# RWKV-6 attention and a SiLU block on one core: the fourth unit takes its near-diagonal scores as matmul levels, not elementwise

## The chip, the cores and the metric

The kernel runs on one core of one Trainium2 chip. The metric is the device time in microseconds (us) of the whole program, a median of several runs. The core has five engines that work side by side, each through its own instructions in order: TensorE (matmuls; PE in the profile, its weight loads PEld), VectorE (DVE), ScalarE (ACT), GpSimd (POOL) and SyncE (SP, which issues the transfers here).

## The reference

Two blocks follow each other. The first is a linear attention with a state that decays by a factor for each channel and token:

```python
for t in range(S):                       # B, H, S, D = 4, 8, 768, 48
    cur = np.einsum('bhd,bhe->bhde', u[None] * kt, vt)
    y[:, :, t] = np.einsum('bhd,bhde->bhe', rt, state + cur)
    state = wt[:, :, :, None] * state + np.einsum('bhd,bhe->bhde', kt, vt)
```

Its output, as a matrix x of 3072 tokens by 384 channels, goes through `h = x @ w_in` (384 by 2048), `g = h / (1 + exp(-h))` (SiLU) and `g @ w_out` (2048 by 384). All is in float32.

## The kernel before

**Units.** A unit is a stretch of 128 tokens of two of the four batch rows; there are 12 (`units`, line 66), numbered 0 to 11. For each unit the attention is computed in chunk form: a 128 by 128 matrix of scores for each head, applied to the values, plus the contribution of the state; then the state is brought forward. The result goes to `xt`, and the SiLU block follows: eight `up` steps (line 920, 12 matmul records each, with one ScalarE activation) and seven `quarter` steps (line 977, 16 records each). The quarters are the second product by a scheme with seven half-size products in place of eight; the scheme needs sums of the activations (`sums`, line 967) and of the weights (`weight_sums`, line 963), and every quarter ends in one or two additions on VectorE at line 1000. Quarter results alternate between two PSUM buffers (`p_o`), so quarter x waits for the addition of quarter x-2.

**Scores by levels.** Token t reads token s before it with the product of all decays between them. The 128 tokens are split by halves: at level l (block size 2 to the l) the second half of each pair of blocks reads the first half. A level takes 16 matmul records (`score_products`, line 661), and a masked copy on VectorE for each of two head groups (`keep_masked`, line 676). Before each level, queries and keys are multiplied by the decay products that take them to their block's edge: `grow_queries` (VectorE), `grow_keys` and `start_keys` (GpSimd), with a ScalarE copy, `odd_keys` or `odd_ones`. `product` (line 405) makes the decay products of the levels on GpSimd. From unit 2 on, two levels run as one burst (`burst`, line 743): `prepare` writes the queries of the second level into another buffer, so that 32 records can run together; `keep_level` then does the masked writes and `go_on` grows keys and queries for what follows. `go_on` and `prepare` need the burst's keys, and their GpSimd work is in order behind whatever else GpSimd was given.

**The diagonal.** The scores nearest the diagonal come in one of two ways, chosen by `NPAIR = 3` (line 69):

- Units 0 to 2: only the pair of tokens (2i, 2i+1) is made elementwise. `bonus` (line 420) is three products on GpSimd, `bonus_sum` (line 434) sums them on VectorE and sends them by four small transfers, `bonus_spread` (ScalarE) and `bonus_write` (VectorE) put them into `score`. The levels 1 to 6 are matmuls.
- Units 3 to 11: whole blocks of 8 tokens are made elementwise, so that only levels 3 to 6 are matmuls. `block_bonus` (line 485) has eight steps of products on GpSimd (all recorded as line 487), `block_sum` (line 519) five of sums on VectorE (line 521); `block_move` sends the sums through DRAM, `block_spread` and `block_write` put them into `score`. Keys and queries are grown in place over levels 0 and 1 by `grow_own` (line 629). These units need their tokens' r, k and w in another layout, which `load_rk` (line 131) brings; `ruk` has one buffer, and the products write over the loaded tokens. `load_u` and `make_block_mask` are done once before the first such unit.

**The order of the work.** It is written out by hand. Units 0 to 2 are lists near the end of the function. From unit 3 on, `mix(i)` (line 867) gives 13 groups, and the loop at line 1093 emits a group, then so many steps of the SiLU block as the table `ROOM` says: the seven quarters of unit i-2 first, then the eight up steps of unit i-1. In `mix`, the first elementwise unit (`first`, i = 3) has its own turns and products within itself, and its elementwise products lie between its levels; it makes steps 0 to 3 of unit 4 (`early`) in its last group, and unit 4 (`second`) has sums 0 and 1 and steps 4 and 5 in its own third group. All later units find steps 0 to 3 made before their turns (group 10 of the unit before), and sums 0 and 1 and steps 4 and 5 in the last group of the unit before. `turns` are the transposes of w, k and r on VectorE (line 360); `turn_k` (line 773) turns the keys back on TensorE.

The loads of the unit after next are dealt out over the groups from 10 on in unit 3, and from 3 on in the later ones. All transfers are issued by SyncE, in the order of emission.

Of the kernel before, what the change touches and what calls it, by code (L numbers as in the profile page):

```python
# [38 lines left out]
def kernel(  # L39
# [16 lines left out]
    NL = 7  # L56
    NB = 2
# [8 lines left out]
    units = [(n, b0) for n in range(S // L) for b0 in range(0, B, NB)]  # L66
    NSLOT = 2
    NTOK = 2
    NPAIR = 3
    FIRST = 3  # L70
    BLK = 1 << FIRST

# [58 lines left out]
    def load_rk(i):  # L131

        if i < NPAIR:
            for x, src in enumerate((r, k)):
# [10 lines left out]
    second = []  # L145
# [131 lines left out]
    room = pt.tile([128, 4, DM // 2], F32, name="partial", bufs=1).rearrange("p x d -> p (x d)")  # L277
# [45 lines left out]
    first = {}  # L323
# [127 lines left out]
    at = 768  # L451
# [409 lines left out]
    def both(fn, i, *args):  # L861
        return [(fn, i, b, *args) for b in range(NB)]

    def block_loads(i):
        return [(load_blocks, i, name, g) for name in "wkr" for g in range(4)]

    def mix(i):

        first, second, later = i == NPAIR, i == NPAIR + 1, i > NPAIR
        ahead = i + 1 < len(units)  # L870

        def at(now, *steps):
            return steps if now else ()

        def bonus_steps(j, *steps):
            return [(block_bonus, j, x) for x in steps]

        def sum_steps(j, *steps):
            return [(block_sum, j, x) for x in steps]

        def turns(j):
            return [*both(turn, j, "w"), (product, j, 0), *both(turn, j, "k"), *both(turn, j, "r"), (grow_own, j, 0)]

        def start(j):
            return [*[(product, j, l) for l in range(1, NL)], (grow_own, j, 1)]

        early = bonus_steps(i + 1, 0, 1, 2, 3)
        middle = [*sum_steps(i + 1, 0, 1), *bonus_steps(i + 1, 4, 5)]
        move = [*sum_steps(i, 3, 4), (block_move, i), *at(ahead, (load_rk, i + 1))]
        groups = [[*at(first, *both(turn, i, "w"), (product, i, 0))],  # L890
                  [*at(first, *both(turn, i, "k"), *both(turn, i, "r"), (grow_own, i, 0))],
                  [*at(first, *start(i)), *at(second, *sum_steps(i, 0, 1), *bonus_steps(i, 4, 5))],
                  [(odd_keys, i, 2), (grow_keys, i, 2, False), (grow_queries, i, 2), *at(later, *sum_steps(i, 2))],
                  [(prepare, i, 3), *at(first, *bonus_steps(i, 0, 1, 2, 3)), *at(later, *bonus_steps(i, 6, 7))],
                  [(burst, i, 3), (keep_level, i, 3), *at(first, *sum_steps(i, 0, 1), *bonus_steps(i, 4, 5)), *at(later, *move)],
                  [(keep_level, i, 4), (go_on, i, 4), *at(first, (make_block_mask,), *sum_steps(i, 2), *bonus_steps(i, 6))],
                  [(prepare, i, 5), (reverse_v, i), *at(first, *bonus_steps(i, 7))],
                  [*at(first, *move), *at(later, (block_spread, i), (block_write, i))],
                  [(burst, i, 5), (keep_level, i, 5), *at(first, (block_spread, i)), (keep_level, i, 6), (go_on, i, 6),
                   *at(first, (block_write, i))],  # L900
                  [*at(later and ahead, *early)],
                  [*at(i < len(units) - NB, *both(turn_k, i)), *at(ahead, *turns(i + 1))],
                  [*both(y_state, i), *both(y, i), *both(update, i), *at(ahead, *start(i + 1)), *at(first, *early),
                   *at(later and ahead, *middle), (move_x, i)]]

        loads = block_loads(i + NSLOT) if i + NSLOT < len(units) else []
        if i + 1 < len(units):
            loads.insert(len(loads) // 2, (load_values, i + 1))

        behind = groups[3 if i > NTOK + 1 else 10:]  # L910
        for at, group in enumerate(behind):
            group += loads[at * len(loads) // len(behind):(at + 1) * len(loads) // len(behind)]
        return groups
# [92 lines left out]
    def ups(i):  # L1006

        steps = [[(up, i, m)] for m in range(FC // 2)]
        for m in range(FH // 2 - 1):

            steps[FH // 2 + 1 + m].append((sums, i, m))
        steps[-1].append((sums, i, FH // 2 - 1))
        return steps

    def downs(i):
        return [[(quarter, i, x)] for x in range(7)]

    def do(*steps):
        for fn, *args in steps:
            fn(*args)  # L1020
# [16 lines left out]
    blocks = block_loads(2)  # L1037
# [30 lines left out]
    blocks = block_loads(3)  # L1068
# [6 lines left out]
    for m in range(6):  # L1075
# [4 lines left out]
    blocks = block_loads(4)  # L1080
    do(*blocks[0:2], (level, 2, 2), (prepare, 2, 3), (weight_sums, 1), (down, 0, 1, 0), (down, 0, 0, 3), (down, 0, 1, 1),
       (sums, 1, 0), (bonus, 2, 0), (bonus_sum, 2, 0))
    do(blocks[2], (burst, 2, 3), (keep_level, 2, 3), (keep_level, 2, 4), (go_on, 2, 4), (prepare, 2, 5), (bonus, 2, 1),
       (bonus, 2, 2), (down, 0, 1, 2), (bonus_sum, 2, 1), (load_rk, 3), (load_u,), (sums, 1, 1), *blocks[3:7], (down, 0, 1, 3))
    do((burst, 2, 5), (keep_level, 2, 5), (keep_level, 2, 6), (go_on, 2, 6), (up, 1, 6), (bonus_spread, 2), (bonus_write, 2),
       (load_values, 3), *both(turn_k, 2), (weight_sums, 2), (up, 1, 7), (sums, 1, 2))
    do((sums, 1, 3), *both(y_state, 2), *both(y, 2), *both(update, 2),
       (move_x, 2),
       *blocks[7:])

    ROOM = 1, 1, 1, 2, 2, 1, 1, 1, 2, 1, 1, 1, 0
    assert sum(ROOM[:5]) >= 7
    for i in range(3, len(units)):
        steps = downs(i - 2) + ups(i - 1)
        groups = mix(i)
        if i == NTOK + 1:

            groups[3].insert(0, (weight_sums, 3))
        for group, room in zip(groups, ROOM):
            do(*group)  # L1100
            for step in steps[:room]:
                do(*step)
            steps = steps[room:]
    for step in downs(len(units) - 2) + ups(len(units) - 1) + downs(len(units) - 1):
        do(*step)

# [29 lines left out]
```

## Time and profile before

| | |
|---|---|
| Time, median of 3 runs | 636.34 us (636.14 to 637.03) |
| Span in the profile | 634.8 us, mean granted TensorE clock 0.997 |
| TensorE busy, matmul / weight load | 620.5 us / 561.6 us |
| VectorE, GpSimd, ScalarE busy | 434.4 us, 373.7 us, 185.8 us |
| Chain that ended last | TensorE 80%, GpSimd 9%, transfers 4%, VectorE 3% |
| Up steps (line 925) | 1152 records, 258.1 us |
| Quarters (line 991) | 528 + 508 + 176 records in the three largest groups, 208.3 us |
| Level matmuls with p_sc (line 669) | 496 records, 36.5 us |
| Block products with ruk from tokens (line 487) | 36 records, 56.3 us |

A line of the page's groups has: source line, engine, operation, output and inputs, shape, count; then the busy time in all, the mean of one in ns, and the engine's idle time just before them with what ended it. A timeline line has: start and length in us, engine, line, operation, count, and in brackets the idle time before with its releaser. One row of the slices has 40 equal slices of the span, each digit the busy share in tenths.

### The profile page before, as it was taken

To read this page: it belongs to the slowest core of one execution; us is meant where nothing else is said; L and a number is where in the kernel's file an instruction comes from. 1 tells how busy PE (TensorE), PEld (TensorE's weight loads), DVE (VectorE), ACT (ScalarE), POOL (GpSimd) and SP (SyncE) were. 2 spreads that over 40 slices of the span, in tenths; PEclk is the share of its full clock that TensorE was granted. 3 is DMA by queue.
4 is the path that set the end of the run, shared out by engine and by line. 5 is a ranking of instruction groups with operands and counts; after the bars stand their busy time and mean duration, and the time that the engine had idled before them with its cause. 6 is when DMAs were issued, how large, how long until landed. Compare 5 with 4: busy or idle time off the path is not lost.

```text
span 634.8 us, 12253 instructions
## 1 busy us (share of the span) xinstructions
PE 620.5 (98%) x4574; PEld 561.6 (88%) x4574; DVE 434.4 (68%) x750; ACT 185.8 (29%) x377; POOL 373.7 (59%) x421
## 2 busy tenths in 40 slices
PE   8999999999888999999999999999999999999997
PEld 7888876889788899899889889989989989989997
DVE  7879779885593696696587596497597587561031
ACT  5798881202310321221221221221131122120120
POOL 6998298569469278478278378468458558500000
PEclk9999999999998999999999999999999999999999
DMA  9966864533353643543443442453353222100000
GB/s 216 290 152 167 190 176 50 112 73 65 81 71 55 128 65 52 126 64 51 111 67 52 110 72 49 96 87 51 79 102 53 47 62 52 34 0 26 26 1 25
DMA packets 203292, 53.75 MB, mean 85 GB/s; under 512 B 186465, under 2 KB 194657, under 8 KB 203233
## 3 DMA queue, kind: packets, MB, share of 16 engines
q1 hardware_dynamic: 201648, 52.39, 40.7%
q10 hardware_dynamic: 1584, 0.59, 0.5%
q8 instruction: 36, 0.59, 0.4%
q14 instruction: 24, 0.19, 0.1%
HBM read 43.67 MB, written 5.31 MB: 77 GB/s over the span
## 4 chain that ended last, share of the span: by engine, by line
PE 80%; POOL 9%; DMA 4%; DVE 3%; SPq 2%; issue 1%; ACT 1%; POOLq 0%; DVEq 0%; ACTq 0%
PE p_h L925 36%; PE p_o L991 27%; PE p_sc L669 4%; PE p_m L807 3%; PE p_m L947 2%; PE p_m L669 2%; PE p_m L794 2%; DMA tokens_w<-in_w_dram 2%; POOL ruk L487 2%; POOL tk L625 2%; POOL tw L408 2%; DMA u_bc<-in_u_dram 1%; POOL tk L634 1%; PE p_m L781 1%; PE p_sc L821 1%
## 5 line engine op out<-in xcount | busy, mean ns | idle before, releaser
L925 PE MATMUL p_h<-xt,w_in_sb 128*128 128x256 f32 x1152 | 258.1, 382 | 0.7 <-POOL tk L649 0.7
L925 PEld LDWEIGHTS p_h<-xt,w_in_sb 128*128 128x128 f32 x1152 | 215.9, 190 | 32.6 <-POOL tk L649 0.9
L934 ACT ACTIVATE gt<-p_h 128x512 f32<-128x512 f32 x90 | 53.6, 596 | 248.2 <-PE p_h L925 248.1
L625 POOL TENSOR_TENSOR tk<-tk,tw 128x256 f32<-128x256 f32 x126 | 86.9, 711 | 60.1 <-ACT tk L595 31.3
L991 PE MATMUL p_o<-own,temps 128*128 128x192 f32 x528 | 90.5, 331 | 5.8 <-DVE temps L1000 3.7
L991 PEld LDWEIGHTS p_o<-own,temps 128*128 128x128 f32 x528 | 87.6, 193 | 7.2 <-DVE temps L1000 4.6
L991 PE MATMUL p_o<-w_out_sb,gt 128*128 128x192 f32 x508 | 87.4, 328 | 0.0
L991 PEld LDWEIGHTS p_o<-w_out_sb,gt 128*128 128x128 f32 x508 | 82.7, 190 | 0.9 <-issue 0.4
L487 POOL TENSOR_TENSOR ruk<-tokens_rk 128x768 f32<-128x768 f32 (+1 forms) x36 | 56.3, 1574 | 39.4 <-DMA tokens_rk<-in_k_dram 28.2
L408 POOL TENSOR_TENSOR tw<-tw 128x256 f32<-128x256 f32 (+6 forms) x83 | 45.0, 542 | 52.2 <-DVE tw L360 48.3
L973 DVE TENSOR_TENSOR temps<-gt 128x256 f32<-128x256 f32 x84 | 54.7, 651 | 18.3 <-ACT gt L934 18.3
L595 ACT COPY tk<-tk 128x256 f32<-128x256 f32 x51 | 20.6, 403 | 101.6 <-POOL tk L625 71.9
L607 DVE TENSOR_TENSOR tr<-tr,tw 128x512 f32<-128x512 f32 x62 | 47.6, 768 | 3.7 <-POOL tk L625 1.1
L679 DVE COPY_PREDICATED score<-mask,p_sc 128x512 f32<-128x512 int8 x60 | 42.1, 753 | 10.9 <-PE p_sc L669 10.0
L669 PEld LDWEIGHTS p_sc<-tr,tk 48*128 48x128 f32 x496 | 30.4, 187 | 10.1 <-issue 6.6
L669 PE MATMUL p_sc<-tr,tk 48*128 48x128 f32 x496 | 36.5, 285 | 0.7 <-POOL tk L625 0.7
L521 DVE TENSOR_REDUCE block_sums<-ruk 128x4 f32<-128x192 f32 (+1 forms) x54 | 27.1, 542 | 7.5 <-POOL ruk L487 7.5
L1000 DVE TENSOR_TENSOR ob<-p_o,partial 128x192 f32<-128x192 f32 x22 | 7.9, 358 | 35.4 <-PE p_o L991 35.4
L1000 DVE TENSOR_TENSOR temps<-p_o,partial 128x192 f32<-128x192 f32 x22 | 7.9, 358 | 34.9 <-PE p_o L991 24.7
L557 DVE COPY_PREDICATED score<-spare 128x1024 f32<-128x1024 int8 x18 | 30.6, 1752 | 0.3
L991 PE MATMUL p_o<-w_out_sb,temps 128*128 128x192 f32 x176 | 30.4, 326 | 0.0
L487 POOL TENSOR_TENSOR tokens_rk<-tokens_rk,tokens_w 128x192 f32<-128x192 f32 (+1 forms) x36 | 29.4, 838 | 1.4
(170 smaller groups left out, 825.9 us busy)
## 6 DMA issues: line engine op xcount, KB each, us to landing
w_out_sb<-in_moe_w_in_dram SPq DMA_DIRECT2D x6, 768.0 KB, 8.1
tokens_rk<-in_r_dram SPq DMA_DIRECT2D x9, 384.0 KB, 4.5
tokens_rk<-in_k_dram SPq DMA_DIRECT2D x9, 384.0 KB, 5.5
tokens_w<-in_w_dram SPq DMA_DIRECT2D x9, 384.0 KB, 6.4
w_out_sb<-in_moe_w_out_dram SPq DMA_DIRECT2D x4, 768.0 KB, 6.8
own<-in_moe_w_out_dram SPq DMA_DIRECT2D x4, 768.0 KB, 5.2
xt<-yt SPq DMA_DIRECT2D x60, 48.0 KB, 2.0
raw<-in_w_dram SPq DMA_DIRECT2D x80, 32.0 KB, 2.4
```

What stands on the lines that cost most here:

```text
L408: engine.tensor_tensor(out=up, in0=t[:, :, 0::2], in1=t[:, :, 1::2], op=ALU.mult)
L487: mul = lambda out, one, two: nc.gpsimd.tensor_tensor(out=out, in0=one, in1=two, op=ALU.mult)
L521: add = lambda out, have: nc.vector.tensor_reduce(out=out, in_=have, axis=mybir.AxisListType.X, op=ALU.add)
L557: nc.vector.copy_predicated(out=score[:, i % NSC, e].rearrange("p (b q) (i s) -> p b q i s", b=NB, s=BLK), mask=block_mask[:, :, None].to_ ...
L607: nc.vector.tensor_tensor(out=odd, in0=odd, in1=tw[i][l][:, :, 0::2][:, :, :, None].to_broadcast([128, Q, L >> (l + 1), c]), op=ALU.mult)
L625: nc.gpsimd.tensor_tensor(out=out, in0=have, in1=odd_products(i, l, b, *blocks), op=ALU.mult)
L669: nc.tensor.matmul(bass.AP(tensor=s_p.tensor, offset=s_p.offset, ap=[s_p.ap[0], [apart * L // 2, 2], [1, L // 2]]), lhsT=tk[i][rows, X[l % ...
L679: nc.vector.copy_predicated(out=dst, mask=masks[l][:, :, None].to_broadcast([128, NB, NP, ni, c]), data=sc[e].rearrange("p (b q) (i c) -> ...
L925: nc.tensor.matmul(p_h[:, a, :], lhsT=w_in_sb[:, c, f * 128:(f + 1) * 128], rhs=xt[i][:, c, :], start=(c == 0), stop=(c == KC - 1))
L934: nc.scalar.activation(out=gt[i, m], in_=p_h, func=AF.Silu)
L973: nc.vector.tensor_tensor(out=out, in0=one, in1=two, op=op)
L991: nc.tensor.matmul(p, lhsT=left(f), rhs=right[:, f, :], start=(f == 0), stop=(f == FH - 1))
```

## The change

`NPAIR` becomes 4. Unit 3 is then of the kind of units 0 to 2: levels 1 to 6 as matmuls, now in three bursts (1 and 2, 3 and 4, 5 and 6), the pair diagonal elementwise, with its write (`bonus_write`) behind the keys of level 5. Elementwise blocks of 8 begin with unit 4. `mix` has one list of groups for unit 3, one for the later ones, and a common end: steps 0 to 3 of the next unit before its turns, sums 0 and 1 and steps 4 and 5 in the last group. `load_u` moves from before unit 3 into it, with the row load of unit 4; `make_block_mask` stays in it. The loads of unit 5, emitted in unit 3, are dealt over four groups and not three. The table of room becomes one for each kind; the quarters of unit 1 keep their places ahead of level 3, and unit 3 has four up steps, not five, between its levels 3 and 5.

It is meant to take the elementwise work of the first such unit out of a stretch in which nothing of it can be made ahead, so that the first elementwise unit finds its products begun, like those after it.

The core of the diff:

```diff
-    NPAIR = 3
+    NPAIR = 4
...
-        first, second, later = i == NPAIR, i == NPAIR + 1, i > NPAIR
...
+        end = [[*at(ahead, *bonus_steps(i + 1, 0, 1, 2, 3))],
+               [*at(i < len(units) - NB, *both(turn_k, i)), *at(ahead, *turns(i + 1))],
+               [*both(y_state, i), *both(y, i), *both(update, i), *at(ahead, *start(i + 1)),
+                *at(ahead, *sum_steps(i + 1, 0, 1), *bonus_steps(i + 1, 4, 5)), (move_x, i)]]
+        if i < NPAIR:
+            groups = [[*both(turn, i, "w"), (product, i, 0)],
+                      [*both(turn, i, "k"), *both(turn, i, "r"), (odd_ones, i)], [(start_levels, i), (prepare_keys, i, 1)],
+                      [(prepare, i, 1), *[(product, i, l) for l in range(1, NL)]],
+                      [(burst, i, 1), (keep_level, i, 1), (bonus, i, 0)],
+                      [(keep_level, i, 2), (go_on, i, 2), (bonus_sum, i, 0), (bonus, i, 1), (bonus, i, 2)],
+                      [(prepare, i, 3), (reverse_v, i)],
+                      [(burst, i, 3), (keep_level, i, 3), (bonus_sum, i, 1), (load_rk, i + 1), (load_u,)],
+                      [(keep_level, i, 4), (go_on, i, 4), (make_block_mask,)],
+                      [(prepare, i, 5), (bonus_spread, i), (bonus_write, i)],
+                      [(burst, i, 5), (keep_level, i, 5), (keep_level, i, 6), (go_on, i, 6)], *end]
+        else:
+            groups = [[], [(odd_keys, i, 2), (grow_keys, i, 2, False), (grow_queries, i, 2), *sum_steps(i, 2)],
+                      [(prepare, i, 3), *bonus_steps(i, 6, 7)],
+                      [(burst, i, 3), (keep_level, i, 3), *sum_steps(i, 3, 4), (block_move, i), *at(ahead, (load_rk, i + 1))],
+                      [(keep_level, i, 4), (go_on, i, 4)],
+                      [(prepare, i, 5), (reverse_v, i)],
+                      [(block_spread, i), (block_write, i)],
+                      [(burst, i, 5), (keep_level, i, 5), (keep_level, i, 6), (go_on, i, 6)], *end]
...
-        behind = groups[3 if i > NTOK + 1 else 10:]
+        behind = groups[10 if i < NPAIR else 1:]
...
-       (bonus, 2, 2), (down, 0, 1, 2), (bonus_sum, 2, 1), (load_rk, 3), (load_u,), (sums, 1, 1), *blocks[3:7], (down, 0, 1, 3))
+       (bonus, 2, 2), (down, 0, 1, 2), (bonus_sum, 2, 1), (load_rk, 3), (sums, 1, 1), *blocks[3:7], (down, 0, 1, 3))
...
-    ROOM = 1, 1, 1, 2, 2, 1, 1, 1, 2, 1, 1, 1, 0
...
-            groups[3].insert(0, (weight_sums, 3))
-        for group, room in zip(groups, ROOM):
+            groups[4].insert(1, (weight_sums, 3))
+        room = (1, 1, 0, 2, 1, 1, 1, 1, 1, 2, 2, 1, 1, 0) if i < NPAIR else (3, 2, 2, 1, 1, 1, 2, 1, 1, 1, 0)
```

More of the change, by code (lines that the diff above doesn't have):

```diff
@@ L885, in start @@
             return [*[(product, j, l) for l in range(1, NL)], (grow_own, j, 1)]
[L887 to L904, printed above, removed]
@@ L1089 @@
        *blocks[7:])
-    ROOM = 1, 1, 1, 2, 2, 1, 1, 1, 2, 1, 1, 1, 0
-    assert sum(ROOM[:5]) >= 7
     for i in range(3, len(units)):
@@ L1096 @@
         if i == NTOK + 1:
-            groups[3].insert(0, (weight_sums, 3))
-        for group, room in zip(groups, ROOM):
+            groups[4].insert(1, (weight_sums, 3))
+        room = (1, 1, 0, 2, 1, 1, 1, 1, 1, 2, 2, 1, 1, 0) if i < NPAIR else (3, 2, 2, 1, 1, 1, 2, 1, 1, 1, 0)
+        for group, count in zip(groups, room):
             do(*group)
-            for step in steps[:room]:
+            for step in steps[:count]:
                 do(*step)
-            steps = steps[room:]
+            steps = steps[count:]
     for step in downs(len(units) - 2) + ups(len(units) - 1) + downs(len(units) - 1):
```

## The prediction

> **What bounds the kernel now.** I read the page first (busy shares, slices), then the chain of waits, then the timeline of TensorE from 128 to 206 us, then those of GpSimd and VectorE over the same stretch.
>
> ```profile
> PE 620.5 (98%) x4574; PEld 561.6 (88%) x4574; DVE 434.4 (68%) x750; ACT 185.8 (29%) x377; POOL 373.7 (59%) x421
> ...
> PE   8999999999888999999999999999999999999997
> ...
> PEclk9999999999998999999999999999999999999999
> ```
>
> TensorE is busy for 98% of the span and is the bound, except in slices 11 to 13 (eights, about 159 to 206 us), where one slice also has a lower granted clock. That is unit 3, the first elementwise one, and the start of unit 4. The timeline of TensorE there (start, length, then the group, in brackets the idle time before it and its releaser):
>
> ```profile
> 137.35 5.47 PE L991 MATMUL p_o<-own,temps 128*128 128x192 f32 x32 [1.27 <-DVE temps L1000]
> ...
> 163.08 1.16 PE L669 MATMUL p_sc<-tr,tk 48*128 48x128 f32 x16
> ...
> 172.11 1.24 PE L781 MATMUL p_m<-ident,tk 128*128 128x128 f32 x8 [1.60 <-DVE score L679]
> ...
> 180.26 5.47 PE L991 MATMUL p_o<-w_out_sb,gt 128*128 128x192 f32 x32
> 185.56 2.90 PE L991 MATMUL p_o<-own,temps 128*128 128x192 f32 x16
> 190.46 2.87 PE L991 MATMUL p_o<-own,temps 128*128 128x192 f32 x16 [2.00 <-DVE temps L1000]
> 195.43 4.55 PE L991 MATMUL p_o<-own,temps 128*128 128x192 f32 x16 [2.10 <-DVE partial L1000]
> ...
> 205.11 1.16 PE L669 MATMUL p_sc<-tr,tk 48*128 48x128 f32 x16
> ```
>
> A unit without waits is one whole period: in the chain of waits the pair of bursts at level 5 begins at 318.52, 367.26 and 416.00 us, 48.75 us apart. The pairs of units 3 and 4 begin at 163.08 and 220.31, which is 57.23. So 8.5 us are lost there: 1.6 at the transpose of the keys (172.11), and at the seven quarters of the output product (180.26 to 205.11, 24.85 us against 18.46 from 284.92 to 303.38 two units later) 6.4. The quarters of unit 4 to 5 (235.46 to 254.64) take 19.18, so 0.7 is lost there too. The wait of 1.27 at 137.35 is a further loss, ahead of this pair.
>
> Why the quarters wait: the timeline of VectorE shows their additions (L1000) queued behind sums of the elementwise diagonal, which wait for GpSimd.
>
> ```profile
> 193.60 0.95 DVE L521 TENSOR_REDUCE block_sums<-ruk 128x16 f32<-128x768 f32 x1 [3.19 <-POOL ruk L487]
> 194.56 0.56 DVE L521 TENSOR_REDUCE block_sums<-spare 128x8 f32<-128x384 f32 x1
> 195.03 0.35 DVE L1000 TENSOR_TENSOR partial<-p_o,partial 128x192 f32<-128x192 f32 x1
> ...
> 197.99 1.13 DVE L521 TENSOR_REDUCE block_sums<-ruk 128x4 f32<-128x192 f32 x4 [1.84 <-POOL ruk L487]
> ```
>
> GpSimd starts unit 4's diagonal products only at 189.43, after the state and all products of the decays, since `early` for unit 4 stands in the last group of unit 3. In the later units they run before the turns (267.26 for unit 6) and the same sums wait for nothing.
>
> [...] two waits of 2 us close together, and the 16 matmuls at 195.43 span 4.55 us against 2.76 elsewhere. [...] here 16 level matmuls of 48 rows take 1.09 us on the chain, though each lasts 272 ns. [...] The six decay products of unit 3 take 4.91 us on GpSimd (136.32) beside the weight sum on VectorE (L965), against 2.91 in unit 4[...].
>
> **The change part by part.**
>
> *Levels 1 and 2 of unit 3 on TensorE (added).* One more burst: 1.09 + 0.89 = 1.98 us, as each burst on the chain. All of it is on the bound.
>
> *Masked writes of these levels (added), VectorE.* Four copies at about 0.65 us, 2.6. VectorE has gaps of 1 to 2.2 us between the quarters' additions from 142.85 to 149.14; hidden.
>
> *Elementwise products of unit 3 (removed), GpSimd.* The rows of L487 from 146.17 to 164.0: 1.81+1.82+1.01+1.00+2.43+0.59+1.70+1.82+1.81 = 14.0 us. In their place three pair products as unit 2 has them: 1.18 (L428), 2.26 (L430), 2.14 (L432). Also grow_own at levels 0 and 1 (1.64+1.44) makes way for four start_keys (0.66 each from L649) and grow_keys at 1 (1.22).
>
> *Where that leaves the bursts.* The quarters start at 128.0 as before. Quarter 3 needs the addition of quarter 1, which no longer stands behind grow_queries at level 0 (0.86 us, 136.05): it starts near 136.45, so 0.9 of the wait is saved, and ends at 139.1. Burst 1 needs keys: key turn done at 134.8, start_keys to 137.45, the ScalarE copy of odd keys (0.41) to 138.0, grow_keys to 139.3, needed for level 2 only at 140.2. No wait. Then quarters 4 to 6 take TensorE to 149.0 and level 3 to 150.05. On GpSimd after grow_keys: the decay products 139.3 to 142.2 or 144, the first pair product, grow_keys at 2 to about 146.4. The second pair product overwrites `ruk`, which the VectorE sum of the first still reads; that sum stands behind the write of level 2 and grow_queries and ends near 147.3. Then 3.65 us (two 768-element products undisturbed, 1.81+1.82) or 4.4 (unit 2's), and only behind them grow_keys at 3 (1.22): keys of level 4 at 152.2 to 152.9. TensorE waits in level 4 for 2.2 to 2.9 us; I take 2.5. If GpSimd were free of these three it would be zero, and that is the other bound.
>
> *Burst at 5 of unit 3.* It now follows four up steps, not five, at 153.4 + 10.5 = 163.9. Its keys have no bonus products ahead of them and are done by 158. The diagonal: SyncE is occupied with loads to 155.14 and two outputs, the four small transfers take 2.84 us of issue (as at 116.95) and land about 1.8 us later, near 160.5; five ScalarE copies (1.0), then the write of 2.5 us on VectorE ends by 164.5. Queued behind the ScalarE copies are the activations of up 2 and 3, for which TensorE's up 4 waits, but only from 165.9: 4 us to spare. Writes of levels 5 and 6 end near 167.7; the key transpose comes three up steps later, at 173.8, so the wait of 1.60 at 172.11 (with its restart 1.7) is gone.
>
> *Unit 4's elementwise start (moved ahead).* Steps 0 to 3 now stand ahead of the turns of unit 4, steps 4 and 5 in unit 3's last group. Tokens: issued at about 159, landing within 6.3 us, so steps 0 to 3 (5.7 to 7.5 us) run from about 167 to 174 on GpSimd, just before the first product of the turn. The addition of quarter 1 comes after turns, sums of the up steps (5.2), the state (1.1), grow_queries and two block sums, near 187; it is needed at 189.8. So no wait, as in unit 6: the 6.4 us go. This part carries the forecast.
>
> *Unit 5.* Its tokens are asked for with unit 4's block_move, issued 7.5 us after burst 3 (212.63). In the new order SyncE is less behind; I take half of the 0.7 lost, 0.4.
>
> *Free.* The row load for unit 3 is four transfers in place of three, and without the decays; it has 20 us until the first pair product. load_u, the mask and the move of x lie beside matmuls. Units 5 and later keep their order and their room.
>
> Sum: +1.98 + 2.5 − 0.9 − 1.7 − 6.4 − 0.4 = −4.9. 636.34 − 4.9 = 631.4 us.
>
> **The rivals.** *No key wait*: the pair products end before TensorE needs level 4, because the sum of the first comes sooner or TensorE comes later. For it: all its figures are within 3 us. Against: `ruk` has one buffer. 631.4 − 2.5 = 628.9. *Unit 4 stays partly late*: tokens of unit 4 land late behind the block loads (issued one after another on SyncE, 0.5 to 0.6 us each), steps 0 to 3 delay the first product and half of the 6.4 remains. For it: in unit 5 the same step waited 7.21 us for its tokens and lost 0.7; against: that lateness cost only 0.7. 631.4 + 3.2 = 634.6. *Slower*: GpSimd becomes the bound of unit 3: burst 1 waits 1.5 for keys[...], level 4 waits 3.5, and unit 4's start is pushed so that it loses the old 6.4. 636.34 + 1.98 + 1.5 + 3.5 − 2.6 = 640.7. For it: two of unit 3's three bursts follow close on GpSimd; against: GpSimd has some 8 us less to do in this unit.
>
> **How the numbers follow.** Forecast 0.56; no key wait 0.20; partly late 0.14; slower 0.10. The likeliest gives 631.4. The low end is no key wait with all of unit 5's loss gone, 628.9 − 0.3 = 628.6; the high end is the partly late case, 634.6. Faster by over 0.2% (below 635.1) holds in the first three but for an edge: 0.88; same 0.03; slower 0.09.
>
> **What would show it.** In the new profile: a burst of 32 level matmuls near 139 us; a wait of 2 to 3 us in the burst at 3, between its levels, released by GpSimd tk L625; no wait at the key transpose; the seven quarters of unit 4 in about 18.5 us at full clock with L487 of unit 4 before its turns. The pair of bursts at 5 of unit 4 would begin near 216 in place of 220.31, and from there 48.8 us per unit. The prediction is wrong if the quarters after unit 3 still wait on additions behind block sums, or if unit 3 waits for anything over 3 us.

## The result and the profile after

The changed kernel takes 632.16 us (median of 4 runs, 631.27 to 632.84) against 636.24 of the kernel before on the same occasion: a ratio of 0.9934, 95% interval 0.9916 to 0.9951. That is 4.1 us less; 4.9 less was forecast. On the chip of the first experiments it ran again: 632.76 against 636.0, ratio 0.9946 (0.9933 to 0.9958).

The page of the changed kernel: busy times, then the slices of TensorE and of its granted clock.

```profile
PE 621.7 (99%) x4606; PEld 563.5 (89%) x4606; DVE 434.8 (69%) x749; ACT 187.2 (30%) x380; POOL 364.5 (58%) x414
...
PE   8999999998999999999999999999999999999997
...
PEclk9999999998999999999999999999999999999999
```

The three eights of before (slices 11 to 13) have become one, in slice 10, and the lower clock has moved there with it. The timeline of TensorE, changed kernel:

```profile
135.98 2.87 PE L995 MATMUL p_o<-own,temps 128*128 128x192 f32 x16 [0.38 <-DVE temps L1004]
138.78 1.18 PE L669 MATMUL p_sc<-tr,tk 48*128 48x128 f32 x16
...
148.77 1.16 PE L669 MATMUL p_sc<-tr,tk 48*128 48x128 f32 x16
151.92 1.86 PE L669 MATMUL p_m<-tr,tk 48*128 48x128 f32 x16 [1.98 <-POOL tk L625]
153.71 11.55 PE L929 MATMUL p_h<-xt,w_in_sb 128*128 128x256 f32 x48
...
175.05 1.04 PE L781 MATMUL p_m<-ident,tk 128*128 128x128 f32 x8
...
182.99 5.47 PE L995 MATMUL p_o<-w_out_sb,gt 128*128 128x192 f32 x32
188.30 7.96 PE L995 MATMUL p_o<-own,temps 128*128 128x192 f32 x48
...
201.39 1.16 PE L669 MATMUL p_sc<-tr,tk 48*128 48x128 f32 x16
```

The added burst stands at 138.78. Level 4 waits 1.98 us for keys in the burst at level 3; its 16 records then span 1.86 us (1.06 elsewhere) and the four up steps 11.55 (four times 2.63 is 10.5). The granted clock is 0.58 over those 16 records, 0.63 over the 2.6 us after them and 1.00 from 156.30 on; in the kernel before it is 0.61 from 195.43 to 199.82. There is no wait at the key transpose (175.05), and the seven quarters of unit 4 (those that run among unit 4's steps) run through: 182.99 to 201.39, 18.40 us for 24.85 before.

Between the same marks of the two profiles: from the first of the quarters in unit 3 (128.01 before, 127.53 now) to the first in unit 4, 55.46 us for 52.25, so +3.2; unit 4's quarters, -6.45; unit 5's, 18.39 for 19.1, -0.7; all that follows, the same within 0.1 us. With the 0.5 by which this profile was already earlier at the first mark, -4.4, which is the difference of the spans (634.8 and 630.4).

The lines of VectorE that answer to those of before:

```profile
186.56 0.94 DVE L521 TENSOR_REDUCE block_sums<-ruk 128x16 f32<-128x768 f32 x1
187.43 0.54 DVE L521 TENSOR_REDUCE block_sums<-spare 128x8 f32<-128x384 f32 x1
188.55 0.36 DVE L1004 TENSOR_TENSOR temps<-p_o,partial 128x192 f32<-128x192 f32 x1 [0.59 <-issue]
```

The sums wait for nothing, and the addition is done before its matmuls need the buffer. This looks as if the earlier products of unit 4 were the cause, as the prediction said. The experiments say otherwise.

### The profile page after: what moved, and what is told of

Read it like the earlier page. It is cut to its first block, busy times and chain, and to the rows that moved or that the text cites. A ratio compares the mean times of both kernels' runs of the same rounds, so it can differ in the third digit from the quotient of the medians.

```text
span 630.4 us, 12322 instructions
## 1 busy us (share of the span) xinstructions
PE 621.7 (99%) x4606; PEld 563.5 (89%) x4606; DVE 434.8 (69%) x749; ACT 187.2 (30%) x380; POOL 364.5 (58%) x414
## 4 chain that ended last, share of the span: by engine, by line
PE 92%; DVE 3%; POOL 2%; ACT 1%; DMA 1%; issue 1%; SPq 0%; POOLq 0%; DVEq 0%; ACTq 0%
PE p_h L929 40%; PE p_o L995 31%; PE p_sc L669 5%; PE p_m L951 3%; PE p_m L807 3%; PE p_m L669 3%; PE p_m L794 3%; PE p_m L781 1%; PE p_sc L821 1%; DMA raw<-in_r_dram 1%; POOL tk L625 1%; PE p_m L845 0%; DVE score L584 0%; DVE tr L607 0%; POOL w_in_sb L241 0%
## 5 line engine op out<-in xcount | busy, mean ns | idle before, releaser
L995 PE MATMUL p_o<-own,temps 128*128 128x192 f32 x528 | 88.1, 326 | 0.4 <-DVE temps L1004 0.4
L995 PEld LDWEIGHTS p_o<-own,temps 128*128 128x128 f32 x528 | 86.0, 190 | 0.8 <-DVE temps L1004 0.7
L487 POOL TENSOR_TENSOR ruk<-tokens_rk 128x768 f32<-128x768 f32 (+1 forms) x32 | 51.4, 1616 | 38.7 <-DMA tokens_rk<-in_k_dram 26.1
L977 DVE TENSOR_TENSOR temps<-gt 128x256 f32<-128x256 f32 x84 | 52.8, 629 | 19.0 <-ACT gt L938 19.0
L679 DVE COPY_PREDICATED score<-mask,p_sc 128x512 f32<-128x512 int8 x62 | 44.5, 772 | 15.3 <-PE p_sc L669 14.7
L1004 DVE TENSOR_TENSOR partial<-p_o,partial 128x192 f32<-128x192 f32 x33 | 11.7, 354 | 28.4 <-PE p_o L995 28.4
L995 PEld LDWEIGHTS p_o<-w_out_sb,temps 128*128 128x128 f32 x176 | 28.9, 190 | 0.0
L487 POOL TENSOR_TENSOR tokens_rk<-tokens_rk,tokens_w 128x192 f32<-128x192 f32 (+1 forms) x32 | 27.5, 878 | 1.3
```

The costliest lines, as they stand in the source:

```text
L487: mul = lambda out, one, two: nc.gpsimd.tensor_tensor(out=out, in0=one, in1=two, op=ALU.mult)
L679: nc.vector.copy_predicated(out=dst, mask=masks[l][:, :, None].to_broadcast([128, NB, NP, ni, c]), data=sc[e].rearrange("p (b q) (i c) -> ...
L977: nc.vector.tensor_tensor(out=out, in0=one, in1=two, op=op)
L995: nc.tensor.matmul(p, lhsT=left(f), rhs=right[:, f, :], start=(f == 0), stop=(f == FH - 1))
L1004: nc.vector.tensor_tensor(out=to, in0=p, in1=known, op=ALU.add)
```

## The experiments

**The wait inside unit 3.** The timeline of GpSimd, changed kernel, gives the chain ahead of level 4's keys: the second pair product waits for the VectorE sum of the first, the third follows, and only then come the keys.

```profile
146.64 1.81 POOL L430 TENSOR_TENSOR ruk<-tokens_rk 128x768 f32<-128x768 f32 x1 [1.31 <-DVE own_sums L437]
148.53 2.14 POOL L432 TENSOR_TENSOR ruk<-ruk,u_bc 128x768 f32<-128x768 f32 x1
150.63 2.52 POOL L625 TENSOR_TENSOR tk<-tk,tw 128x256 f32<-128x256 f32 x4
```

Three variants of the changed kernel, on one chip with it.

> The changed kernel once more, beside the three variants of it. All theories: 632.2 us, with a wait of about 2 us between level 3 and level 4 of unit 3 on TensorE, and slower matmuls after it.

Measured: 632.76 us; a wait of 1.98 us, and the up steps after it span 12.27 us.

```diff
-                      [(keep_level, i, 2), (go_on, i, 2), (bonus_sum, i, 0), (bonus, i, 1), (bonus, i, 2)],
-                      [(prepare, i, 3), (reverse_v, i)],
+                      [(keep_level, i, 2), (go_on, i, 2), (bonus_sum, i, 0)],
+                      [(prepare, i, 3), (bonus, i, 1), (bonus, i, 2), (reverse_v, i)],
```

> The second and third pair product of unit 3 behind the keys of level 4 on GpSimd; nothing else moves. Theory of the key chain (level 4's keys wait behind the products, which wait for the one ruk buffer): no wait between levels 3 and 4, 1.98 us of idle time gone and the 0.97 and 0.96 us by which level 4 and the four up steps were slowed, in all 3.9, so 628.3 us. Rival (level 4 is held by its queries or its score buffer, GpSimd only comes last by a little): a wait of 1 us or more is left and the time stays above 630.5 us.

Measured: 629.09 us, ratio to the kernel before 0.9885 (0.987 to 0.9901); 3.7 less than the changed kernel. The timeline of TensorE of this variant:

```profile
149.66 1.16 PE L669 MATMUL p_sc<-tr,tk 48*128 48x128 f32 x16
150.65 1.06 PE L669 MATMUL p_m<-tr,tk 48*128 48x128 f32 x16
151.64 10.63 PE L929 MATMUL p_h<-xt,w_in_sb 128*128 128x256 f32 x48
```

No wait, and no slow matmuls behind it. On GpSimd the keys of levels 3 and 4 follow each other at once (144.91), and the products come after. The key chain is the cause.

```diff
-                      [(keep_level, i, 2), (go_on, i, 2), (bonus_sum, i, 0), (bonus, i, 1), (bonus, i, 2)],
+                      [(bonus_sum, i, 0), (keep_level, i, 2), (go_on, i, 2), (bonus, i, 1), (bonus, i, 2)],
```

> The VectorE sum of the first pair product ahead of the masked write of level 2 and grow_queries, so that ruk comes free earlier; GpSimd's order stays. Theory of the key chain: GpSimd starts the second product at about 145.4 in place of 146.64 us, the wait in the burst shrinks from 1.98 to about 0.75 us; 630.9 us if the clock still drops, 629.0 us if the shorter wait spares it. Rival (ruk has no part in it, GpSimd is late by its own load): the wait stays at 2 us, 632.2 us.

Measured: 629.93 us, ratio 0.9903 (0.989 to 0.9917), 2.8 less than the changed kernel. The second product now starts at 145.49 without a wait, so `ruk` was indeed what it waited for. The wait of TensorE is 1.10 us, and what follows runs at full pace:

```profile
151.23 1.16 PE L669 MATMUL p_m<-tr,tk 48*128 48x128 f32 x16 [1.10 <-POOL tk L625]
152.32 10.63 PE L929 MATMUL p_h<-xt,w_in_sb 128*128 128x256 f32 x48
```

0.9 us less of waiting gave 2.8 us. The rest came with the matmuls behind the wait: 1.16 and 10.63 us for 1.86 and 11.55, the mean granted clock of the runs 0.999 to 1.0 for 0.997. The next variant tests whether the wait is what lowers the clock, by filling it with useless work.

```diff
-        score_products(i, l, before.pop((i, l)), made[i, l])
+        queries = before.pop((i, l))
+        for _ in range(2 if (i, l) == (3, 3) else 1):
+            score_products(i, l, queries, made[i, l])
```

> TensorE computes level 3 of unit 3 twice (16 more matmul records, 1.09 us of useless work that gives the same scores), in the place where it waits for the keys of level 4. Theory that the idle time costs more than itself through the clock: idle time falls to about 0.9 us, the clock stays full, and the time falls by up to 1.9 us, to 630.3, although more is done. Rival (the slower matmuls after the wait have another cause): unchanged, 632.2. Rival (the added work is on the bound): 633.3.

Measured: 631.26 us (630.83 to 632.24), 1.5 less than the changed kernel, with 16 matmul records more. The wait is 1.11 us, and level 4 (1.16) and the up steps (10.63) are at full pace. The clocks agree: the mean granted clock is 0.997 in all five runs of the changed kernel beside these variants, and 0.999 or 1.0 in every run of the three. So this wait of 1.98 us cost about 3.5 in all: itself, and 1.5 (this variant) to 1.9 (2.8 less 0.9, the one before) for the lower clock behind it.

**What took away unit 4's 6.4 us.** Two runs on one chip split the change into its halves. First, the order alone: the kernel before, unit 3 elementwise, with unit 4's steps in the new places.

```diff
-                  [*at(first, *start(i)), *at(second, *sum_steps(i, 0, 1), *bonus_steps(i, 4, 5))],
+                  [*at(first, *start(i))],
...
-                  [*at(later and ahead, *early)],
+                  [*at(ahead, *early)],
...
-                  [*both(y_state, i), *both(y, i), *both(update, i), *at(ahead, *start(i + 1)), *at(first, *early),
-                   *at(later and ahead, *middle), (move_x, i)]]
+                  [*both(y_state, i), *both(y, i), *both(update, i), *at(ahead, *start(i + 1)),
+                   *at(ahead, *middle), (move_x, i)]]
```

> The kernel before with only the order of unit 4's elementwise work as in the change: steps 0 to 3 before the turns of unit 4, sums 0 and 1 and steps 4 and 5 in the last group of unit 3; unit 3 stays elementwise. My theory (order and early tokens are both needed): the tokens of unit 4 are still asked for at 168.4 us and land near 175, so steps 0 to 3 end near 183 and push unit 4's first product and state update some 3 us back; VectorE's addition of quarter 1 comes near 192 where 188 is needed: about 4 of the 6.4 us stay lost, 633.5 us. Rival (the order alone is the gain, the pair unit only costs): 629.5 us.

Measured: 639.83 us, ratio 1.0056 (1.0043 to 1.0068). Both theories miss: the order alone makes the kernel slower. The timeline of VectorE of this run, the first sums of the up steps:

```profile
175.77 2.02 DVE L973 TENSOR_TENSOR temps<-gt 128x256 f32<-128x256 f32 x1
177.82 1.93 DVE L973 TENSOR_TENSOR temps<-temps,gt 128x256 f32<-128x256 f32 x1
179.67 1.23 DVE L973 TENSOR_TENSOR temps<-gt 128x256 f32<-128x256 f32 x1
180.82 1.23 DVE L973 TENSOR_TENSOR temps<-gt,temps 128x256 f32<-128x256 f32 x1
181.97 0.41 DVE L973 TENSOR_TENSOR temps<-gt 128x256 f32<-128x256 f32 x1
```

Steps 0 to 3 run on GpSimd from 174.94 to 181.77; beside them each sum takes 1.2 to 2.0 us, and 0.41 as soon as they end. The turns of unit 4 begin at 183.44 in place of 178.37. All that follows on VectorE is later by as much: TensorE waits 1.37 and 1.27 us for sums of the up steps (190.40 and 192.59), and 3.33 us for the addition of quarter 1 (196.83). The seven quarters take 26.84 us (182.27 to 209.11), 2.0 more than in the kernel before.

That is not all of the loss. The key transpose, ahead of the first moved step, waits longer than in the kernel before (2.12 us for 1.60), and the matmuls after it are slow:

```profile
172.44 1.49 PE L781 MATMUL p_m<-ident,tk 128*128 128x128 f32 x8 [2.12 <-DVE score L679]
173.72 4.23 PE L925 MATMUL p_h<-xt,w_in_sb 128*128 128x256 f32 x12
```

From the first quarter in unit 3 to the first in unit 4 this run takes 54.47 us (127.80 to 182.27) for 52.25, another 2.2; unit 5's quarters give 0.7 back.

Second, the pair unit alone: the changed kernel with unit 4's steps in the old places.

```diff
-        end = [[*at(ahead, *bonus_steps(i + 1, 0, 1, 2, 3))],
+        late = i < NPAIR
+        end = [[*at(ahead and not late, *bonus_steps(i + 1, 0, 1, 2, 3))],
...
-                *at(ahead, *sum_steps(i + 1, 0, 1), *bonus_steps(i + 1, 4, 5)), (move_x, i)]]
+                *at(late, *bonus_steps(i + 1, 0, 1, 2, 3)),
+                *at(ahead and not late, *sum_steps(i + 1, 0, 1), *bonus_steps(i + 1, 4, 5)), (move_x, i)]]
...
+        if i == NPAIR:
+            groups[0:1] = [[], [], [*sum_steps(i, 0, 1), *bonus_steps(i, 4, 5)]]
```

> The changed kernel with unit 4's elementwise work in the old order: steps 0 to 3 at the end of unit 3's last group, sums 0 and 1 and steps 4 and 5 in unit 4 after two quarters; unit 3 stays a pair unit with three bursts. My theory: the quarters of unit 4 wait for block sums as before, 6.4 us, and unit 5 loses its 0.7 again: 638.6 to 639.3 us, slower than before. Rival (the pair unit relieves GpSimd, and the order matters little): 632 to 633 us.

Measured: 633.22 us, ratio 0.9954 (0.994 to 0.9968), where 638.6 to 639.3 was expected. My theory falls. The timeline of TensorE of this run:

```profile
183.95 5.47 PE L999 MATMUL p_o<-w_out_sb,gt 128*128 128x192 f32 x32
189.25 7.96 PE L999 MATMUL p_o<-own,temps 128*128 128x192 f32 x48
```

And that of VectorE:

```profile
175.72 1.30 DVE L360 STREAM_TRANSPOSE tw<-raw 128x512 f32<-128x512 f32 x2
...
191.20 0.95 DVE L521 TENSOR_REDUCE block_sums<-ruk 128x16 f32<-128x768 f32 x1 [1.33 <-POOL ruk L487]
192.15 0.56 DVE L521 TENSOR_REDUCE block_sums<-spare 128x8 f32<-128x384 f32 x1
192.62 0.35 DVE L1008 TENSOR_TENSOR partial<-p_o,partial 128x192 f32<-128x192 f32 x1
```

The block sums wait for GpSimd as they did in the kernel before, and the addition stands behind them, and yet no quarter waits: the buffer is needed only at about 194.5 (two quarters of 2.6 us after 189.25). What differs is where VectorE stands. In this run the turns of unit 4 (the first of them is the transpose of w, L360) begin at 175.72, the key transpose of TensorE is at 176.00. In the kernel before they begin at 178.37, 6.3 us after the key transpose (172.11). The timeline of VectorE of the kernel before:

```profile
171.12 0.01 DVE L551 LOAD_MASK_SELECT spare<-spare  x1 [4.83 <-ACT spare L550]
...
173.07 2.49 DVE L557 COPY_PREDICATED score<-spare 128x1024 f32<-128x1024 int8 x2
...
178.37 1.30 DVE L360 STREAM_TRANSPOSE tw<-raw 128x512 f32<-128x512 f32 x2
...
190.05 0.36 DVE L1000 TENSOR_TENSOR temps<-p_o,partial 128x192 f32<-128x192 f32 x1
```

GpSimd is late with it, since its first decay product waits for that turn (it starts at 179.75 before and at 177.09 in this run): the products of unit 4's diagonal begin at 189.43 in the kernel before, and at 187.01 in this run, though TensorE's quarters begin 3.7 us later here.

New theory: unit 3's diagonal comes back late from its way through DRAM, VectorE waits for it ahead of the write of level 6, and is 6 us late from there on. To test it, the two steps that bring the diagonal in are left out for unit 3 of the kernel before; its near-diagonal scores are then missing. This takes away the wait (4.83 us) and VectorE's own work on the diagonal (about 2.7) together.

```diff
-                  [(burst, i, 5), (keep_level, i, 5), *at(first, (block_spread, i)), (keep_level, i, 6), (go_on, i, 6),
-                   *at(first, (block_write, i))],
+                  [(burst, i, 5), (keep_level, i, 5), (keep_level, i, 6), (go_on, i, 6)],
```

> The kernel before without the spread and the masked write of unit 3's diagonal (two steps left out for this one unit, so its near-diagonal scores are not those of the reference); products, sums and transfers stay, and unit 4's elementwise steps keep the old order. New theory (the 6.4 us come from VectorE, which reaches unit 4's turns some 6 us after TensorE's key transpose because unit 3's diagonal comes back late): the turns begin near 172 us in place of 178.4, no wait at the key transpose, the quarters of unit 4 wait for 0 to 1.5 us in all: 628 to 630 us. Rival (my first theory, the late products of unit 4 on GpSimd): only the 1.7 us at the key transpose go, the quarters still take near 25 us: 634 to 635 us.

Measured: 636.18 us, ratio 1.0 (0.9992 to 1.0008). Neither theory. In the trace the local part is as expected: the turns begin at 170.92 (7.45 us earlier), 0.6 us after the key transpose (170.34), which does not wait, and the quarters take 19.16 us (178.28 to 197.44), so that burst 3 of unit 4 is 7.7 us earlier than in the kernel before. Then the gain is given back: TensorE waits 3.95 us for an activation, and the 24 records after it span 7.66 us where 5.45 is usual. The timelines of TensorE, of ScalarE and of SyncE of this run, in this order:

```profile
218.58 7.66 PE L924 MATMUL p_h<-xt,w_in_sb 128*128 128x256 f32 x24 [3.95 <-ACT gt L933]
```

```profile
216.39 0.24 ACT L548 COPY spare<-spare 128x64 f32<-128x64 f32 x1 [8.29 <-DMA spare<-kept]
```

```profile
212.45 0.42 SPq L540 DMA_DIRECT2D kept<-block_sums  x1
```

The activations that free the up steps' buffers stand on ScalarE behind the copies of unit 4's diagonal, and those wait for transfers that SyncE issued at 212.45 us, as late as in the kernel before (212.63), though the last block sum is ready at 201.64. SyncE is working off loads without a gap up to then. It had stood idle before, from 156 to 165 us, since the transfer of unit 3's block sums is in front of the loads in its queue and waits for them.

So there are two bounds, one behind the other. The last two runs test this: the loads of unit 5 dealt out from unit 3's group 5 on, so that SyncE issues 16 of them in its idle time; once on top of the run above, once on the kernel before as it is.

```diff
-        behind = groups[3 if i > NTOK + 1 else 10:]
+        behind = groups[5 if i == NPAIR else 3:]
```

> The kernel before without the spread and write of unit 3's diagonal (as in the run before it, near-diagonal scores of this unit are left out), and with the loads of unit 5 dealt over unit 3's groups from 5 on and not from 10 on, so that SyncE issues 16 of them in the 9 us in which it stood idle for unit 3's block sums (156 to 165 us). Theory of two bounds (VectorE late in unit 3, and behind it SyncE's queue, which sends unit 4's block sums at 212.5 us though they are ready at 201.6): unit 4's diagonal goes out near 204 us, the wait of 3.95 us of TensorE on ScalarE with the slow matmuls after it, and the 1.4 of unit 5, are gone: 628.5 to 630 us. Rival (something else holds unit 4's diagonal): 635 to 636.5 us as without the early loads.

Measured: 628.51 us, ratio 0.9876 (0.9863 to 0.989). Unit 4's block sums go out at 204.96, TensorE does not wait there, and the whole gain comes through.

> The kernel before, all of it, with only the loads of unit 5 dealt over unit 3's groups from 5 on. Theory of two bounds: the waits of unit 3 and of unit 4's quarters (1.7 and 6.4 us) stay, since they come from VectorE; SyncE is 9 us less behind in unit 4, which is worth at most the 0.7 of unit 5: 635.5 to 636.5 us. Rival (SyncE's queue alone is the bound): 628 to 632 us.

Measured: 635.92 us, ratio 0.9997 (0.9989 to 1.0006). The loads alone give nothing that can be told from no change: the waits of VectorE's making stay, as this timeline of TensorE shows.

```profile
190.49 2.87 PE L991 MATMUL p_o<-own,temps 128*128 128x192 f32 x16 [2.00 <-DVE temps L1000]
195.47 4.55 PE L991 MATMUL p_o<-own,temps 128*128 128x192 f32 x16 [2.11 <-DVE partial L1000]
```

In this trace the quarters of unit 5 take 18.4 us (235.49 to 253.89), so the 0.7 lost there before came from SyncE being behind.

In the changed kernel unit 3 has no block sums. VectorE still waits for its pair diagonal (5.35 us), but that wait ends at 162.52, before the matmuls of level 5 (165.19), and the turns begin at 174.76, just ahead of the key transpose (175.05). SyncE's queue is not held either: the tokens of unit 4 are asked for at 155.89 in place of 168.44, and unit 4's block sums go out at 205.62. By these traces the pair unit lifts both bounds at once.

**The rest.** Two runs on one chip ask what the new order is worth once unit 3 no longer waits: the variant with the later pair products, with the old and with the new order of unit 4.

> The pair unit with the old order of unit 4's elementwise work, and with unit 3's second and third pair product behind the keys of level 4. If the order of unit 4 is worth nothing where VectorE is early: the same as its twin with the new order, 629.1 us within 0.5. If it hides a small gain: 0.5 to 1.5 us above the twin.

> The changed kernel with the second and third pair product of unit 3 behind the keys of level 4, once more, as the twin on the same chip: 629.1 us.

Measured: 628.94 us with the old order, ratio 0.9881 (0.9866 to 0.9896); 628.60 with the new, 0.988 (0.9866 to 0.9893). The order of unit 4's steps is worth nothing that can be measured. The version with the later pair products beats both kernels.

And the order alone with three of unit 4's early products left out, to see whether GpSimd's products are what slows VectorE's sums:

```diff
-        early = bonus_steps(i + 1, 0, 1, 2, 3)
+        early = bonus_steps(i + 1, *((0,) if first else (0, 1, 2, 3)))
```

> The order alone on the kernel before, with steps 1, 2 and 3 of unit 4's products left out (three GpSimd instructions of 1.9, 1.2 and 1.1 us; unit 4's diagonal is then not the reference's). Theory ([...] the sums take 7.3 us in place of 2.9 and the turns come 5 us later): most of the sums take 0.42 us each again, the turns begin near 179 us, and the time falls to 633 to 635 us. Rival (the sums are slow or late for another cause): 639.8 us as with all products.

Measured: 637.30 us, ratio 1.0017 (1.0009 to 1.0025). The sums are as expected: one of 2.03 us beside the product that is left, then 0.42 each. The time is 2.5 less than with all products but 2.3 above the range expected. So the three products account for 2.4 of the 3.5 us (3.5 less the 1.1 that is left here). The turns begin at 180.47, and the additions still stand behind the block sums in this order, so a quarter waits 3.32 us at 193.88. Yet the seven quarters take 23.62 us (182.40 to 206.02), less than the 24.85 of the kernel before. What is longer in this trace is again the key transpose: it waits 2.02 us, the 12 records after it span 3.98 us where 2.75 is usual, and from the first quarter in unit 3 to the first in unit 4 this trace takes 2.1 us more. Why this wait is above 2 us in both runs with the new order alone, though it stands ahead of the moved steps, was not tried and stays open.

## Why the prediction was right, and where it was wrong

The size was right (4.1 measured, 4.9 forecast), the steps in part. With the costs that the runs showed the prediction's sum is 1.98 + 3.7 − 0.9 − 1.7 − 6.4 − 0.7 = −4.0.

*Levels 1 and 2*: 1.99 us (138.78 to 140.77), forecast 1.98. Right. *Quarter 3's wait*: from 1.27 to 0.38, forecast 0.9 less. Right. *Key transpose*: no wait. Right.

*Wait for level 4's keys*: mechanism right, down to the single buffer of `ruk`; 1.98 us of idle time, under the 2.2 to 2.9 given. But the term was mis-sized: the prediction counted the wait alone, and the lower clock behind it (0.58 over level 4) cost 1.5 to 1.9 more. Its cost was 3.7 by the runs (632.76 less 629.09), not 2.5. The prediction had noted slow matmuls behind two such waits in the kernel before and left them out of the sum without giving a reason.

*Unit 4's start*: the 6.4 us went, but the step "This part carries the forecast" names the wrong cause. I had compared unit 4 with unit 6 and put the difference down to the order of the elementwise steps, since the page and the timeline name GpSimd as releaser of the sums in front of the additions. That fits only the second of the two waits (195.43). The first (190.46) ended with the addition at 190.05, which stands ahead of the block sums and behind nothing that waits for GpSimd: VectorE only came to it late, and the prediction passed over that. The old order with a pair unit has no wait in the quarters, and the new order without one is 3.5 us slower. The cause was VectorE's position, 6 us late by unit 3's own diagonal, with SyncE's queue as a second bound behind it. That the number came out is luck: unit 6, which served as the pattern, has no such lateness either (turns at 277.69, key transpose at 276.97).

*Unit 5*: 0.7 where 0.4 was taken, and SyncE's queue as its cause was right. What the prediction did not see is that the same queue would have held unit 4 as well if only VectorE had been freed.

*Hidden work*: the diagonal's write on VectorE took 5.34 us, not 2.5, beside GpSimd's steps 0 to 3 of unit 4, which ran from 162.29 to 170 and not from about 167, and 2.49 in the run where these come later. It ended at 168.06 and not at 164.5; the three up steps ahead of the key transpose still covered it.

## What to carry to other kernels

A queue that waits is late for two possible reasons: what it waits for is late, or it got there late. Measure each engine's distance to the bound engine at the same step (here turns against key transpose) in a good and in a bad period before putting a wait down to the releaser that the trace names. When one wait is lifted and the time stays, look for work that kept its old time of issue: here SyncE issued nothing from 156 to 165 us, with the transfer of unit 3's block sums ahead of the loads, and unit 4's block sums, ready at 201.64, went out at 212.45 behind those loads. And a wait of TensorE is to be priced together with the pace of the matmuls behind it: the one of 1.98 us cost 3.7 here.

## What the runs showed of the hardware that was not expected

After some single waits of about 2 us, TensorE's matmuls ran slower in these profiles. The waits of 1.98, 1.99, 2.02 and 2.12 us are such: in the changed kernel the first 16 records took 1.86 us where 1.06 is usual, at a granted clock of 0.58; after the 1.99 of the pair unit alone they took 1.56, and the four up steps behind them 11.87 where 10.63 is usual; after the waits of 2.02 and 2.12 the 12 records of an up step took 3.98 and 4.23 where 2.76 is usual. So are the waits of 2.10 and 2.11 that came five us after one of 2.00 (16 records in 4.55 for 2.76; granted clock 0.61 behind the 2.10), and the longer ones of 3.33 (32 records in 7.15 for 5.47) and 3.95 (24 in 7.66 for 5.45).

The waits of 1.10, 1.11, 1.27, 1.40 and 1.60 were not followed by slower matmuls: four up steps in 10.63 us behind the first two, 32 records in 5.47 behind the next two, an up step in 2.75 behind the 1.60. Of those at 2 us neither were the first quarter waits of 2.00 in the kernel before and in the early loads alone (16 records in 2.87 behind each, as behind the wait of 0.38 in the changed kernel; granted clock 1.00 in the kernel before), nor the 2.05 at the key transpose of the latter (an up step in 2.75). The same kernel does not always show it either: of the first four runs of the changed kernel one has a mean granted clock of 1.0, the others 0.997, and it took 631.27 us, 0.9 less than the middle one of the others. Why some waits near 2 us are followed by a lower clock and others are not stays open.

Useless matmuls in such a wait made the kernel 1.5 us faster: 631.26 us for 632.76, with a wait of 1.11 us for 1.98.

Beside GpSimd's products, VectorE's sums of the up steps and its masked writes took between two and five times as long as without: a sum of 0.41 us took 2.02 in the order alone, and the pair of writes of 2.49 in the pair unit alone took 5.34 in the changed kernel. With three of the four products left out, one sum beside the product that is left took 2.03 and the others were back at 0.42. By what means was not shown; the size of it, for an engine that is busy for 69% of the span, was not expected.
